# Largest value over the partitions by TensorE and VectorE in place of GpSimd's collective, in a chain of attention, Fourier transforms and two FFNs

## The chip, the cores and the metric

One core of one Trainium2 chip. The time is device microseconds (us) of one execution of the program; three runs of the kernel before gave 1623.56, 1623.72 and 1625.95, so 1623.72 is the median that everything is compared with. PE is TensorE, DVE VectorE, ACT ScalarE, POOL GpSimd, SP SyncE.

## The reference

```python
def _attn_ref(q, k, v):                       # 8 batches, 8 heads, 576 tokens, d = 64
    q_s = np.exp(q - np.max(q, axis=-1, keepdims=True))
    q_s = q_s / (np.sum(q_s, axis=-1, keepdims=True) + 1e-09)
    k_s = np.exp(k - np.max(k, axis=2, keepdims=True))
    k_s = k_s / (np.sum(k_s, axis=2, keepdims=True) + 1e-09)
    kv = np.einsum('bhsd,bhse->bhde', k_s, v)
    return np.einsum('bhsd,bhde->bhse', q_s, kv)

def _moe_ref(x, w_ch1, w_ch2):                # x: [8, 576, 512]
    u = x + np.real(np.fft.fft(np.fft.fft(x, axis=1), axis=2))
    mu = np.mean(u, axis=-1, keepdims=True)
    var = np.mean((u - mu) ** 2, axis=-1, keepdims=True)
    un = (u - mu) / np.sqrt(var + 1e-06)
    return u + np.maximum(un @ w_ch1, 0.0) @ w_ch2          # 512 to 2048 to 512

def _moe2_ref(x, mu_k, mu_r, w_k, w_v, w_r):
    x_prev = np.concatenate([np.zeros((B, 1, D)), x[:, :-1, :]], axis=1)
    xk = mu_k * x + (1.0 - mu_k) * x_prev
    xr = mu_r * x + (1.0 - mu_r) * x_prev
    k = np.maximum(xk @ w_k, 0.0)
    return 1.0 / (1.0 + np.exp(-(xr @ w_r))) * (k * k @ w_v)
```

The weights of the first FFN come as float64. The two maxima that matter here are the one of k over the sequence (`axis=2`), and one that the reference doesn't have: the largest weight of W1 and of W2, by which the kernel chooses a power of two to scale the weights with.

## The kernel before, in words

**Attention** goes by batch b and half hf (four heads each), sixteen halves, in `attention(b)`. In `kt` (k) the 128 partitions are rows of the sequence, so the largest k of a column is a maximum along the free dimension (`tensor_reduce` L313, and two small ones L316 for the last 64 rows) and then one over the partitions (L317, a collective of GpSimd, in place in `m`, all partitions get the result). Beside it q's softmax runs over d, in the free dimension: L321 maximum, L323 subtraction, L324 exponential, L333 to L337 the division by the sum. k less its maximum is L327 and L330, its exponential L331; L342 and L343 make k'v on TensorE in a PSUM bank, L345 to L353 divide it (`kvbd`), L376 transposes q, L395 multiplies q with `kvbd`, L396 writes the result to `U[b]`. Which halves use GpSimd for a subtraction is written in the tables POOL_Q (q less its largest) and POOL_K (k less its largest).

**Transform** (`transform(b)`): even and odd parts (L429 to L445), a product over the features (L474) and one over the sequence (L494 to L498, "stage 2"), whose results are added to `u` in L507 to L517. L517 is the last instruction of a batch's transform.

**Norm** (`norm(i)`): layer norm by blocks of 512 tokens, nine blocks; block 1 needs the transforms of batches 0 and 1. Block 0 goes in two parts of 256 tokens. For block 1 GpSimd adds (L571, L573, L589, L590) and multiplies with the reciprocal deviation (L623); L637 makes the low half of the f16 pair (`unh`, `unl`) that the products read.

**Weights**: `largest` finds the maximum of the absolute value of a piece along the free dimension (L193); `scales(w)` takes the maximum over the pieces (L202), the one over the partitions (L203, the collective again), and makes powers of two (L204 to L209). `split(w, c)` decodes a piece of float64 to float32 on VectorE and GpSimd (L229, L230, GpSimd's L232, L234) and writes two f16 parts (ACT's L243, L246 and L247; L244 on VectorE or L248 on GpSimd).

**FFN**: for each block 16 times `mm1` (L825, three f16 products) and `mm2` (L845), L830 and L831 between them, and L863 adds the result to `u`. In block 0 the products wait for the pieces of weights as they come.

**Order.** Three strands (attention; transform and norm; weights) are written as generators, of which `side()` takes a piece after every few products. The order on each engine comes from a scheduler with a timeline of its own, so the rows of an engine are not in the order of the code; each engine executes its rows in order. Marks (BEHIND_X, BEHIND_Z, BEHIND_S) hold pieces back behind a point of the first batch. Beside the products the strands have two PSUM banks (`side`); the first batch, before the products, also uses one of `acc0` to `acc3`. After the ninth block comes the last part (L887 to L913), which is products throughout.

Of the kernel before, what the change touches and what calls it, by code (L numbers as in the profile page):

```python
# [8 lines left out]
F32 = mybir.dt.float32  # L9
# [5 lines left out]
ALU = mybir.AluOpType  # L15
AX = mybir.AxisListType

S = 576          # tokens of a batch
DM = 512         # model width
HALF = 288       # S / 2  # L20
NK = 258         # cosine columns: k = 256, 0..255 and one of zeros
NS = 290         # s' = 0..288 and one of zeros
RAW = 3          # chunks of the last part's weights that are under way
# Halves (batch, half) of the attention whose steps GpSimd takes: q less its largest, q times its
# reciprocal sum, k less its largest; and halves and weights that come after a mark of the first batch.
POOL_Q = ((0, 0), (1, 0), (2, 0))
POOL_M = ((2, 0),)
POOL_K = ((0, 1), (1, 0))
# [3 lines left out]
# Blocks whose norm GpSimd multiplies, and blocks that are waited for least: their sums on TensorE and in float32.  # L32
# [3 lines left out]
# Rows j of the folded sequence, by tile, of the even and the odd part. The last tile of the even part  # L36
# starts with rows that the tile before has too, where its tables are zero.
JT = (((0, 128), (128, 128), (225, 64)), ((0, 128), (128, 128), (256, 32)))
# 2^-100, the high word of its float64 read as float32
# [4 lines left out]
def net(ctx, tc, q, k, v, w1, w2, mu_k, mu_r, w_k, w_v, w_r, ce_d, se_d, cs_d, ss_d, alt_d, id_d, out):  # L44
# [19 lines left out]
    def aside(first):  # L64
        """A bank beside the products; before those begin, one of theirs too."""
        if not first:
            return bank("side", 2)
        turn_of[0] += 1
        x = turn_of[0] % 6
        return bank("side", 2) if x in (0, 3) else bank(f"acc{(1, 2, 4, 5).index(x)}", 1)  # L70
# [3 lines left out]
    def segments(i):  # L74
        """The batches that a block of tokens covers: batch, first row, rows, place in the block."""
# [9 lines left out]
    # ------------------------------------------------------------------ pools of the first part  # L85
# [20 lines left out]
    ident = fc.tile([128, 128], F32, name="ident")  # L106
    ceh = fc.tile([128, 2, NK], F32R, name="ceh")
# [11 lines left out]
    def load_constants():  # L119
        # They pass where W1 will lie.  # L120
# [8 lines left out]
    def first_constants():  # L129
        st = fw.tile([128, NS], F32, tag="pc", name="st")[:, 0:128]  # L130
        nc.vector.memset(st, 1.0 / DM)
        nc.gpsimd.memset(wsc[:, 7:8], 1e-6)
# [9 lines left out]
    # ------------------------------------------------------------------ weights of the FFN  # L142
    def load_weight(pool, src, t, c, bufs):
        """256 columns of 128 rows of a float64 weight, as its words."""
# [903 lines left out]
```

## Time and profile before

| what | number |
|---|---|
| median of 3 runs | 1623.72 us |
| span of the profiled execution (first to last instruction) | 1622.4 us |
| own time of the profiled execution | not given; the median is 1.3 us above the span |
| PE busy | 1485.2 us (92%) |
| DVE busy | 885.7 us (55%) |
| ACT busy | 576.7 us (36%) |
| POOL busy | 181.8 us (11%) in 188 instructions |
| mean granted TensorE clock | 0.958 |

Busy shares are means over stages that differ: PE is at 26% to 60% of the slices in the first eighth of the span, then at 90% or more to the end. What a change in the first eighth is worth has to be read there, engine by engine, in order of time. One thing isn't counted as busy on POOL: before a collective and again before the next ordinary instruction the engine stands still (idle "<-issue", or put down to an instruction long done). In the program's order these places have an `ISA` row without operands.

### The profile page before, as it was taken

To read this page: it belongs to the slowest core of one execution; us is meant where nothing else is said; L and a number is where in the kernel's file an instruction comes from. 1 tells how busy PE (TensorE), PEld (TensorE's weight loads), DVE (VectorE), ACT (ScalarE), POOL (GpSimd) and SP (SyncE) were. 2 spreads that over 40 slices of the span, in tenths; PEclk is the share of its full clock that TensorE was granted. 3 is DMA by queue.
4 is the path that set the end of the run, shared out by engine and by line. 5 is a ranking of instruction groups with operands and counts; after the bars stand their busy time and mean duration, and the time that the engine had idled before them with its cause. 6 is when DMAs were issued, how large, how long until landed. Compare 5 with 4: busy or idle time off the path is not lost.

```text
span 1622.4 us, 17906 instructions
## 1 busy us (share of the span) xinstructions
PE 1485.2 (92%) x7044; PEld 944.9 (58%) x7044; DVE 885.7 (55%) x1473; ACT 576.7 (36%) x1010; POOL 181.8 (11%) x188
## 2 busy tenths in 40 slices
PE   2644667999999999999999989999999999999999
PEld 2533444454555555555555434446888888888887
DVE  3685879945647547546553896513334443434432
ACT  2563545423323323233232342313334333433421
POOL 1102535302010020020010210000000000000000
PEclk7766889999999999999999999999999999999999
DMA  8363333201201102102010232101001101100000
GB/s 351 130 227 122 133 109 135 87 1 46 72 1 58 61 1 72 46 6 84 30 52 1 97 109 80 52 1 52 26 27 52 48 5 52 53 26 26 27 26 26
DMA packets 41408, 105.99 MB, mean 65 GB/s; under 512 B 5323, under 2 KB 11628, under 8 KB 40300
## 3 DMA queue, kind: packets, MB, share of 16 engines
q1 hardware_dynamic: 41324, 104.85, 18.1%
q8 instruction: 55, 0.90, 0.2%
q14 instruction: 29, 0.24, 0.0%
HBM read 85.96 MB, written 18.87 MB: 65 GB/s over the span
## 4 chain that ended last, share of the span: by engine, by line
PE 76%; DVE 7%; issue 1%; POOL 1%; ACT 1%; DMA 1%; SPq 0%; DVEq 0%; ACTq 0%
PE h L825 19%; PE acc L845 18%; PE acc L913 12%; PE h L898 12%; PE h L887 6%; PE side L474 2%; PE side L494 2%; PE side L342 1%; PE side L395 1%; DVE eo L429 1%; DVE hl L831 1%; PE side L498 0%; PE side L376 0%; DVE words L230 0%; DVE u L863 0%
## 5 line engine op out<-in xcount | busy, mean ns | idle before, releaser
L825 PE MATMUL h<-unh,w1h 128*128 128x512 f16 (+1 forms) x608 | 226.9, 373 | 23.6 <-ACT w1h L247 20.3
L825 PE MATMUL h<-unh,w1l 128*128 128x512 f16 (+1 forms) x608 | 225.5, 373 | 24.0 <-POOL w1l L248 23.7
L825 PE MATMUL h<-unl,w1h 128*128 128x512 f16 (+1 forms) x608 | 226.8, 373 | 0.0
L845 PE MATMUL acc<-hl,w2h 128*128 128x512 f16 x576 | 220.3, 383 | 0.5 <-DVE hl L831 0.5
L845 PE MATMUL acc<-hh,w2l 128*128 128x512 f16 x576 | 219.9, 382 | 0.0
L845 PE MATMUL acc<-hh,w2h 128*128 128x512 f16 x576 | 212.8, 382 | 5.1 <-ACT hh L830 5.0
L825 PEld LDWEIGHTS <-w1h 128*128 128x128 f16 x1216 | 120.0, 99 | 154.6 <-ACT w1h L247 21.6
L845 PEld LDWEIGHTS <-w2h 128*128 128x128 f16 x1152 | 112.1, 99 | 137.9 <-issue 9.5
L913 PE MATMUL acc<-wvh,kk 128*128 128x512 f32 x576 | 190.6, 395 | 0.0
L831 DVE SCALAR_TENSOR_TENSOR hl<-h,hh 128x512 f16<-128x512 f32 x144 | 98.7, 686 | 166.7 <-ACT hh L830 166.1
L898 PE MATMUL h<-x,wkh 128*128 128x512 f32 x576 | 180.8, 395 | 0.0
L830 ACT ACTIVATE hh<-h 128x512 f16<-128x512 f32 x144 | 85.1, 592 | 227.9 <-PE h L825 227.6
L903 DVE SCALAR_TENSOR_TENSOR ke<-h,ke 128x512 f32<-128x512 f32 x72 | 49.7, 690 | 177.8 <-ACT ke L902 177.7
L913 PEld LDWEIGHTS acc<-wvh,kk 128*128 128x128 f32 x576 | 108.1, 188 | 26.3
L898 PEld LDWEIGHTS h<-x,wkh 128*128 128x128 f32 x576 | 108.1, 188 | 26.2
L913 PE MATMUL acc<-wvl,kk 128*128 128x512 f32 x288 | 113.7, 395 | 0.0
L898 PE MATMUL h<-x,wkl 128*128 128x512 f32 x288 | 113.7, 395 | 0.0
L825 PEld LDWEIGHTS <-w1l 128*128 128x128 f16 x608 | 60.1, 99 | 88.5 <-POOL w1l L248 25.6
L902 ACT ACTIVATE ke<-h 128x512 f32<-128x512 f32 x72 | 42.9, 596 | 175.8 <-PE h L898 175.8
L845 PEld LDWEIGHTS <-w2l 128*128 128x128 f16 x576 | 56.8, 99 | 66.2 <-issue 3.3
L887 PE MATMUL h<-wrh,x 128*128 128x512 f32 x288 | 92.1, 396 | 0.0
L699 DVE TENSOR_TENSOR x<-aa,x 128x512 fp32r<-128x512 f32 x72 | 47.8, 687 | 72.0 <-PE h L887 62.4
(290 smaller groups left out, 2251.9 us busy)
## 6 DMA issues: line engine op xcount, KB each, us to landing
raw<-in_w_dram SPq DMA_DIRECT2D x22, 512.0 KB, 3.4
vt<-in_v_dram SPq DMA_DIRECT2D x16, 650.0 KB, 5.8
kt<-in_k_dram SPq DMA_DIRECT2D x16, 576.0 KB, 4.0
qt<-in_q_dram SPq DMA_DIRECT2D x16, 576.0 KB, 3.7
out_dram<-oo SPq DMA_DIRECT2D x36, 256.0 KB, 2.2
y<-yT SPq DMA_DIRECT2D x8, 1026.0 KB, 5.0
w2h<-in_w_dram SPq DMA_DIRECT2D x8, 1024.0 KB, 7.4
w2l<-in_w_dram SPq DMA_DIRECT2D x8, 1024.0 KB, 8.3
```

Source lines behind the costliest of these rows:

```text
L474: mm(out=pt, lhsT=a[:, e, g, js], rhs=c[:, g, :], start=first, stop=(e == 1 and g == 1 and a is el))
L494: mm(out=pt, lhsT=a[:, i, cols], rhs=c[:, i, :], start=(i == 0 and c is ch and a is yh), stop=False)
L699: nc.vector.tensor_tensor(out=l[:, t, 0:n], in0=a, in1=h[:, t, 0:n].bitcast(F32), op=ALU.subtract)
L825: mm(out=pt[:, o:o + m], lhsT=a[:, t, fs], rhs=c[:, t, o:o + m], start=(t == 0 and a is w1h and c is xh), stop=(t == 3 and a is w1l))
L830: nc.scalar.activation(out=hh[:, 0:n], in_=pt[:, 0:n], func=AF.Relu)
L831: nc.vector.scalar_tensor_tensor(out=hl[:, 0:n], in0=pt[:, 0:n], scalar=0.0, in1=hh[:, 0:n], op0=ALU.max, op1=ALU.subtract)
L845: mm(out=acc[x][:, 0:n], lhsT=a[:, f, xs], rhs=c[:, 0:n], start=(f == 0 and a is w2h and c is hh), stop=(f == NF - 1 and a is w2l))
L887: mm(out=pt[0:m, :], lhsT=a[:, t, o:o + m], rhs=c[:, t, :], start=(t == 0 and a is rh and c is wrh), stop=(t == 3 and a is rl))
L898: mm(out=pt[:, 0:n], lhsT=a[:, t, fs], rhs=c[:, t, 0:n], start=(t == 0 and a is wkh and c is kh), stop=(t == 3 and a is wkl))
L902: nc.scalar.activation(out=kr[:, 0:n], in_=pt[:, 0:n], func=AF.Relu)
L903: nc.vector.scalar_tensor_tensor(out=kr[:, 0:n], in0=pt[:, 0:n], scalar=0.0, in1=kr[:, 0:n], op0=ALU.max, op1=ALU.mult)
L913: mm(out=acc[x][0:m, :], lhsT=a[:, o:o + m], rhs=c[:, f, :], start=(f == 0 and a is h2 and c is wvh), stop=(f == NFK - 1 and a is l2))
```

## The change

For batches 0, 1 and 2 (`MAX_PE`) the maximum of k over the partitions is no longer a collective. Two TensorE transposes bring `m` (128 x 256) into a PSUM bank with the columns on the partitions; VectorE takes the maximum along the free dimension (128 x 2); VectorE multiplies an identity matrix with these (128 x 256, two diagonal matrices); a product with a matrix of ones gives every partition all 256 maxima, in the other half of the same PSUM bank, where the subtraction reads them. GpSimd can't do that subtraction here, so POOL_K is empty: the k subtractions of halves (0, 1) and (1, 0) move from GpSimd to VectorE. `scales` does the same in three steps: a diagonal matrix from the 128 maxima, the product with ones, and a maximum along the free dimension. Batches 3 to 7 keep the collective. A new 128 x 128 tile `one` and its memset are added; comments are dropped.

```diff
-POOL_K = ((0, 1), (1, 0))
+POOL_K = ()
...
+MAX_PE = (0, 1, 2)
...
     ident = fc.tile([128, 128], F32, name="ident")
+    one = fc.tile([128, 128], F32, name="one")
...
         nc.vector.memset(st, 1.0 / DM)
+        nc.vector.memset(one, 1.0)
...
         nc.vector.tensor_reduce(out=m, in_=amax[:, w, :], axis=AX.X, op=ALU.max)
-        nc.gpsimd.partition_all_reduce(out_ap=inv, in_ap=m, channels=128, reduce_op=bass_isa.ReduceOp.max)
+        dg = fw.tile([128, NS], F32, tag="pc", name="dg")[:, 0:128]
+        ts(out=dg, in0=ident, scalar1=m, scalar2=None, op0=ALU.mult)
+        pt = aside(False)[:, 0:128]
+        mm(out=pt, lhsT=one, rhs=dg, start=True, stop=True)
+        nc.vector.tensor_reduce(out=inv, in_=pt, axis=AX.X, op=ALU.max)
...
-            nc.gpsimd.partition_all_reduce(out_ap=m, in_ap=m, channels=128, reduce_op=bass_isa.ReduceOp.max)
+            if b in MAX_PE:
+                pt = aside(b == 0)
+                for x in range(2):
+                    nc.tensor.transpose(out=pt[:, 128 * x:128 * x + 128], in_=m[:, 2 * x:2 * x + 2, :], identity=ident)
+                mx = wsc[:, 2:6:3, None]
+                nc.vector.tensor_reduce(out=mx[:, :, 0], in_=pt[:, 0:256].rearrange("p (x c) -> p x c", x=2), axis=AX.X, op=ALU.max)
+                dg = m.rearrange("p h d -> p (h d)").rearrange("p (x c) -> p x c", x=2)
+                tt(out=dg, in0=ident[:, None, :].to_broadcast([128, 2, 128]), in1=mx.to_broadcast([128, 2, 128]), op=ALU.mult)
+                mm(out=pt[:, 256:512], lhsT=one, rhs=dg.rearrange("p x c -> p (x c)"), start=True, stop=True)
+                m = pt[:, 256:512].rearrange("p (h d) -> p h d", h=4)
+            else:
+                nc.gpsimd.partition_all_reduce(out_ap=m, in_ap=m, channels=128, reduce_op=bass_isa.ReduceOp.max)
```

The scheduler orders the engines anew. Three places follow; the changed kernel's lines are 21 further down in the attention (L327 there is L348, L345 is L366), 9 in `split` (L232 is L241, L248 is L257) and 21 after that.

On GpSimd, from the first collective of the first batch to the weights. Before, the first three halves:

```order
L317 ISA
L317 ISA m<-m 128x256
L323 ISA
L323 TENSOR_TENSOR qt<-qt,st 128x1152
L317 ISA
L317 ISA m<-m 128x256
L327 ISA
L327 TENSOR_TENSOR kt<-kt,m 128x1024
L330 TENSOR_TENSOR kt<-kt,m 64x128 x2
```

In the change, from its first such row to the fourth of the weights:

```order
L344 ISA
L344 TENSOR_TENSOR qt<-qt,st 128x1152 x2
L592 TENSOR_TENSOR sq<-u 128x2x64
L241 TENSOR_TENSOR dec<-dec,raw 128x512
L241 TENSOR_TENSOR words<-words,raw 128x512
L241 TENSOR_TENSOR words<-words 128x512
L257 TENSOR_TENSOR w1l<-dec,w1h 128x512
```

One ISA row is left ahead of the weights; the next ones stand at the first collective of batch 3.

On VectorE, the second half of the first batch, in the change (L332 and L334 are the new maximum and the new diagonal matrices, L366 the first step of the division of k'v, L345 before):

```order
L354 TENSOR_REDUCE st<-qt 128x18
L355 TENSOR_SCALAR st<-st 128x18
L356 RECIPROCAL st<-st 128x18
L358 TENSOR_TENSOR qt<-qt,st 128x1152
L332 TENSOR_REDUCE wsc<-acc_199 128x2
L334 TENSOR_TENSOR m<-ident,wsc 128x256
L348 TENSOR_TENSOR kt<-kt,acc_199 128x1024
L351 TENSOR_TENSOR kt<-kt,acc_199 64x128 x2
L366 TENSOR_SCALAR rk<-acc_217 128x2
```

Before, L337 (now L358) was followed by L345 at once: the k subtraction was GpSimd's. Now it stands behind q's division.

On VectorE, the end of the second batch's transform. Before, it lies among the pieces of weights (L244, L229, L230) and block 0's products (L831):

```order
L244 SCALAR_TENSOR_TENSOR w1l<-words,wsc,w1h 128x512
L229 TENSOR_SCALAR dec<-raw 128x512
L507 TENSOR_TENSOR sd<-pc,side 128x290
L508 TENSOR_TENSOR sd<-pc,side 128x290
L229 TENSOR_SCALAR words<-raw 128x512
L230 SCALAR_TENSOR_TENSOR dec<-raw,dec 128x512
L510 TENSOR_TENSOR u<-u,sd 128x2x289
L511 TENSOR_TENSOR u<-u,sd 128x2x287
```

In the change it comes after the last L831 of block 0 (L852 there) and the first two L863 (L884):

```order
L852 SCALAR_TENSOR_TENSOR hl<-h,hh 128x512
L884 SCALAR_TENSOR_TENSOR u<-acc_694,wsc,u 128x512
L884 SCALAR_TENSOR_TENSOR u<-acc_695,wsc,u 128x512
L528 TENSOR_TENSOR sd<-pc,side 128x290
L529 TENSOR_TENSOR sd<-pc,side 128x290
L332 TENSOR_REDUCE wsc<-side 128x2
L884 SCALAR_TENSOR_TENSOR u<-acc_696,wsc,u 128x512
L334 TENSOR_TENSOR m<-ident,wsc 128x256
```

All pieces of weights stand ahead of it. On TensorE stage 2 of the second batch (L494, now L515) likewise comes behind all of block 0's products, among half of which it stood before.

## Rows read from the trace of the kernel before

**Rows 1.** Busy time in stretches: engines, PE clock, DMA share, GB/s
```profile
121.00:152.00 31.00, 7.13 (x39) 5.95 (x40) 14.92 (x34) 7.11 (x10) 9.25 (x9) 0.61 0.17 55
152.00:268.00 116.00, 87.32 (x494) 56.36 (x493) 96.25 (x140) 60.52 (x106) 52.89 (x35) 0.87 0.43 154
...
960.00:1622.00 662.00, 658.64 (x2878) 475.43 (x2877) 273.06 (x453) 224.58 (x380) 6.35 (x64) 1.00 0.11 38
```

**Rows 2.** PE's timeline: first products of block 0 and block 1
```profile
133.34 0.39 PE L825 MATMUL h<-unh,w1h 128*128 128x256 f16 x1 [20.07 <-ACT w1h L247]
...
311.45 0.38 PE L825 MATMUL h<-unh,w1h 128*128 128x512 f16 x1
```

**Rows 3.** PE's waits, 100 to 320 us: total, times, longest
```profile
PE h L825 <- POOL w1l L248: 23.7, 2, 12.2
PE h L825 <- ACT w1h L247: 20.3, 2, 20.1
```

**Rows 4.** GpSimd's timeline, the first batch
```profile
11.25 1.08 POOL L317 PARTITION_ALL_REDUCE m<-m  x1 [9.92 <-issue]
23.18 2.11 POOL L323 TENSOR_TENSOR qt<-qt,st 128x1152 f32<-128x1152 f32 x1 [10.85 <-issue]
35.35 1.08 POOL L317 PARTITION_ALL_REDUCE m<-m  x1 [10.07 <-issue]
43.51 2.33 POOL L327 TENSOR_TENSOR kt<-kt,m 128x1024 f32<-128x1024 f32 x1 [7.07 <-issue]
```

**Rows 5.** DVE's timeline: q's sum (0,0), k'v (0,1), last of block 0, last of transform 1
```profile
26.52 1.35 DVE L333 TENSOR_REDUCE st<-qt 128x18 f32<-128x1152 f32 x1 [9.86 <-ACT qt L324]
...
52.77 0.16 DVE L345 TENSOR_SCALAR rk<-side 128x2 f32<-128x2 f32 x1 [0.45 <-PE side L343]
...
119.96 0.67 DVE L637 TENSOR_TENSOR unl<-d,unh 128x512 f16<-128x512 f32 x1
...
266.48 1.71 DVE L517 TENSOR_TENSOR u<-u,sd 128x574 f32<-128x574 f32 x1
```

**Rows 6.** DVE's waits, 0 to 320 us: total, times, longest
```profile
DVE wsc L204 <- POOL wsc L203: 11.3, 2, 5.9
DVE words L229 <- POOL w1l L248: 10.8, 2, 5.5
DVE kt L327 <- POOL m L317: 9.3, 3, 4.9
DVE w1l L244 <- ACT w1h L243: 5.3, 2, 4.8
DVE dec L229 <- POOL w2l L248: 4.6, 1, 4.6
```

**Rows 7.** GpSimd's timeline, around the collectives of batches 1 and 3
```profile
122.28 1.53 POOL L317 PARTITION_ALL_REDUCE m<-m  x1 [11.51 <-DVE m L316]
130.60 1.26 POOL L232 TENSOR_TENSOR dec<-dec,raw 128x512 uint32<-128x512 uint32 x1 [6.79 <-DVE qt L323]
...
280.56 1.53 POOL L317 PARTITION_ALL_REDUCE m<-m  x1 [7.01 <-DVE m L316]
```

**Rows 8.** Prices: DVE's groups by form, 100 to 320 us (busy, mean ns)
```profile
L831 DVE SCALAR_TENSOR_TENSOR hl<-h,hh 128x512 f16<-128x512 f32 x17 | 11.4, 678 | 1.1 <-ACT hh L830 0.9
...
L313 DVE TENSOR_REDUCE m<-kt 128x256 f32<-128x1024 f32 x5 | 9.6, 1918 | 0.0
...
L327 DVE TENSOR_TENSOR kt<-kt,m 128x1024 f32<-128x1024 f32 x4 | 4.9, 1218 | 5.4 <-POOL m L317 5.4
...
L440 DVE TENSOR_TENSOR eo<-eo 128x289 f32<-128x289 f32 x8 | 3.3, 432 | 0.0
```

**Rows 9.** GpSimd's and DVE's timelines at 174 us, side by side
```profile
174.17 2.11 POOL L323 TENSOR_TENSOR qt<-qt,st 128x1152 f32<-128x1152 f32 x1
174.23 2.33 DVE L229 TENSOR_SCALAR dec<-raw 128x512 uint32<-128x512 uint32 x1 [4.59 <-POOL w2l L248]
...
120.56 0.41 DVE L229 TENSOR_SCALAR dec<-raw 128x512 uint32<-128x512 uint32 x1
```

## The prediction

> **What bounds the kernel now.** I read the busy time in stretches first, then the waits of the engines in the stretches that aren't full. From 960 us on TensorE is busy 658.6 of 662 us [rows 1], and it stays at about 99% from some 315 us: nothing that this change touches lies there, so those 1311 us can only be moved, not shortened. The gain or loss must arise before block 1's first product, at 311.45, which waited for nothing [rows 2]. Between 121 and 152 us TensorE is busy 7.1 of 31 us, at a clock of 0.61; between 152 and 268 it is busy 87 of 116 us while VectorE is busy 96, the fullest engine [rows 1]. The reader is to see a chain of VectorE up to 268 us, with TensorE waiting beside it.
>
> TensorE's own waits say for what: block 0's first product came at 133.34 after 20.1 us on the high half of W1, and 23.7 us went on the low halves that GpSimd writes [rows 2, 3]. GpSimd's timeline says why: every change between the collective and ordinary instructions leaves it standing, some 10 us in the first 36 us (9.92, 10.85, 10.07) and about 7 later (7.07, 6.79, 7.01) [rows 4, 7], while the collective itself takes 1.08 to 1.53 us. I call these gaps loads: in the program's order an ISA row stands at each. VectorE's waits name the same source: 11.3 us for the scales' collective, 10.8 and 4.6 for buffers that GpSimd frees late, 9.3 for k's maximum and 5.3 for ScalarE's w1h [rows 6].
>
> **The change part by part.** I follow VectorE through four points: k'v of half (0, 1) (L345, at 52.77), the last L637 of block 0 (119.96, done at 120.6), the first product (133.34), and the last L517 of the second batch (266.48, done at 268.2) [rows 2, 5].
>
> *The head.* Before, two loads lay ahead of q's subtraction of (0, 0) at 23.18, and two more ahead of the k subtraction at 43.51 [rows 4]. Now one load is left, for the q subtraction itself: it starts where the collective did, 11.3, thus 11.9 earlier, and L333 with it, at 14.6 instead of 26.52 [rows 5]. Then VectorE works in order: 6.1 us of (0, 0) as before, some 4.6 for the maximum, subtraction and exponential of q of (0, 1) (three operations at the 1.35 of L333 or a little less), 3.6 for L333 to L337, which gives 28.9. The maximum and the k subtraction stand behind that. Nothing in the trace shows the new chain; its nearest rows are L440, 0.43 us for 128x289, for each of its two VectorE steps, and 0.39 us for a product of 256 columns [rows 2, 8]. With two TensorE steps that is 1.7 us without and up to 3 us with latencies; I take 2.3, and 1.8 for the subtraction (L327's 1.22 and two of L330): 33.0. What follows the k subtraction until L345 took 6 us before (52.77 less 43.51, less the 3.3 of the subtraction). So L345 comes at about **39.5**, 13 earlier. Bounds: all three loads gone from a pure chain and the rest 11.9 earlier would give 23.7; only one of them off the path, 42.7.
>
> *To the last L637 of block 0*: 67.9 us before. The scale's wait goes (5.4 of the 11.3 [rows 6]; 0.6 of new work comes), and about 4.5 us of the second batch move behind it (one L313 at 1.92 and six small ones at L440's 0.43 [rows 8]). 58.5 remain: T = **98** instead of 120.6.
>
> *To the first product*: 12.7 before, of which 6.79 were the load ahead of L232 [rows 7]. What is left is decode, scaling and rounding, 5 us: **103** instead of 133.3.
>
> *To the end of the transform.* Before, 147.6 us (120.6 to 268.2). VectorE's waits in it that come from loads: 5.9 for the second scale, 10.8 and 4.6 for late buffers, 4.8 of the 5.3 on w1h, 4.9 of the 9.3 on k's maximum [rows 6]: 31 go. Added to VectorE: 4 halves at 0.85 (two steps at 0.43), 0.6 for the scale, 1.8 for half (1, 0)'s k subtraction: 5.7. The 4.5 moved behind come back. And in the new order stage 2 stands behind all pieces of weights and block 0's products: some 15 instructions of 128x512 at 0.68 [rows 8] pass ahead of it, 10 us. That makes 147.6 - 31 + 5.7 + 4.5 + 11 = 138, so the last L517 ends at **236 to 240** instead of 268.2. The pieces go faster for GpSimd too; VectorE stays the fullest engine (96 of 116 us), so I count no more than its own waits.
>
> *Block 1.* Before, its norm took 43.3 us from L517 to the first product, wholly beside block 0's products [rows 2, 5]. Now these are done before, and TensorE stands in the meantime. The chain keeps two loads: the collective of batch 3 stands in it with 7 us on either side [rows 7], since that batch isn't in MAX_PE. I get 41 us (36 if the loads fall beside other steps, 45 if GpSimd's adds queue behind them), and 2 us for products at a lower clock after the gap, as at 0.61 in the stretch before the first product [rows 1]. Block 1 begins at 238 + 41 = 279; its first product then counts as if at about 279.5 against 311.45. That is 32 us.
>
> *The other edits.* TensorE does 20 more small products (about 8 us at most) before 315 us, where it idles; the memset of `one` and the wider use of a bank fall in waits of 10 us at the head. VectorE's extra work, some 10 us in all, is in the sums above. SP's queue gets and loses nothing; loads of q, k and v leave when their buffers come free, which is earlier. The cover for the TensorE work is GpSimd's loads: where they go, it is VectorE's work that covers it.
>
> The sum: the span of 1622.4 less 32 is 1590.4; the median lies 1.3 above the span, so **1591 us** is the time (1591.7 from the sum, rounded down).
>
> The collective's own time is 1.08 to 1.53 us, the new chain's 1.7 to 3: by instruction times alone the change would lose. The Trainium skill says as much: "GPSIMD Engine Reference", section 4.1 "Engine selection", names GpSimd for a reduction along the partition dimension and not VectorE. By that rule the eight replaced collectives would cost about 1.2 us more each. This trace disagrees as far as it goes: 7 to 10 us stand beside each collective here, which the rule doesn't count.
>
> **The rivals.**
> - *More gain.* VectorE's simple operations took 0.41 us alone and 2.33 beside GpSimd [rows 9]; the means of the weights' stage lie between. If, with fewer waits, fewer of them meet, up to 18 us come off the 138: 1573.
> - *Less gain.* The head is set by VectorE and by the arrival of q, k and v rather than by loads: T near 110, or the two `side` banks, of which the maxima of batches 1 and 2 now hold one from the transposes to the subtraction, make products of the transform wait. 12 to 24 of the 32 us go: 1603 to 1615.
> - *The loads were hidden.* If the waits pass on to others (DMA, ScalarE's exponentials), nothing but the order changes: 1620 to 1627. Against it: the load of 6.79 ends at the very instruction whose result TensorE waits for [rows 3, 7].
> - *Only the instructions count.* Six halves and two scales at 1.2 us more each (the chain's middle of 2.4 less the collective's 1.2), on VectorE's path: 9.6 more, 1633.
> - *Slower by a lock.* A VectorE operation that meets a GpSimd instruction with two inputs waits for its end (0.41 against 2.33 [rows 9]). GpSimd has about 64 us of such instructions between T and the last L517; they spread now over a shorter time in which VectorE has no idle places. Some 18 us of it are in today's durations, so at most 46 come on top: L517 at 284, block 1 at 325, time 1637. It decides from 33 of the 46 on; below that the change still wins. The Trainium skill has such a rule: "SBUF — State Buffer", section "Who interferes with whom", has VectorE and GpSimd share a port pair that one instruction holds exclusively. The row at 174.23 agrees; how often they meet isn't shown.
>
> **How the numbers follow.** The forecast (1580 to 1602) gets 0.52, more gain 0.15, less gain 0.22, loads hidden 0.04, instructions only 0.02, the lock 0.05. Faster is the first three, 0.89; same 0.04; slower 0.07 (about 0.2%, 3.2 us, is what a measurement of this kernel can tell from no change). The range from 1568 to 1612 takes in the first two, with their bounds, and most of the third; about 0.18 is left out.
>
> **What would show it.** In the profile of the changed kernel: GpSimd's first ordinary instruction at 11 to 13 us and no gap of 7 us until batch 3's collective; L345's successor of (0, 1) near 39; last low half of block 0 near 98; first product near 103, and no wait of 12 us for low halves; last transform instruction of batch 1 near 238; a wait of 30 us or more on TensorE between block 0's and block 1's products; block 1 at 276 to 284; from there the same 1311 us. A first product before 95 or after 115, a block 1 after 300, or a later part that isn't 1311 us would each prove a step wrong.

## The result, and the profile after

The changed kernel takes 1606.43 us (median of 4 runs, 1604.72 to 1608.45) against 1624.84 of the kernel before in the same runs: a ratio of 0.9882, 95% interval 0.9865 to 0.9898. That is faster by 18 us, clear of the scatter, where 32 were forecast; the time lies inside the range of 1568 to 1612, but above the 1580 to 1602 of the forecast itself, where the rival "less gain" (1603 to 1615) was put. The profiled execution has a span of 1602.9 us and took 1604.7; the span before was 1622.4, so 19.5 us went. TensorE is busy 1489.3 us (1485.2 before), which leaves 113.6 us in which it isn't, against 137.2.

First the busy time in the stretches of [rows 1] (engines PE, PEld, DVE, ACT, POOL, then clock, DMA share, GB/s):

```profile
121.00:152.00 31.00, 21.30 (x118) 14.25 (x115) 29.93 (x47) 15.70 (x25) 13.61 (x10) 0.83 0.41 133
152.00:268.00 116.00, 94.62 (x488) 54.62 (x486) 90.57 (x139) 54.64 (x97) 36.32 (x26) 0.94 0.35 121
268.00:315.00 47.00, 33.84 (x158) 20.35 (x159) 32.39 (x51) 16.84 (x30) 11.76 (x6) 0.79 0.12 40
...
960.00:1602.00 642.00, 639.15 (x2788) 466.61 (x2786) 248.90 (x392) 214.57 (x358) 6.11 (x62) 1.00 0.10 33
```

The hole of 121 to 152 us, with 7.1 us of TensorE, is closed (21.3). A new one stands further on. Here the same view in the stretches that matter now:

```profile
190.00:220.00 30.00, 27.88 (x141) 15.93 (x141) 22.75 (x38) 18.27 (x33) 13.97 (x11) 0.96 0.54 182
220.00:241.00 21.00, 21.00 (x103) 10.99 (x102) 7.62 (x12) 5.73 (x11) 0.07 (x1) 1.00 0.00 1
241.00:253.00 12.00, 10.57 (x67) 8.27 (x65) 9.72 (x19) 3.61 (x5) 0.13 (x1) 1.00 0.24 90
253.00:290.00 37.00, 14.85 (x50) 7.86 (x51) 30.38 (x46) 16.16 (x28) 15.35 (x8) 0.65 0.29 99
```

Up to 220 us every piece of the weights is done (GpSimd's last low half ends at 220.1); from there to 241 TensorE alone is full, at its upper clock, while VectorE is busy 7.6 of 21 us. Then, from 253 to 290, TensorE is busy 14.9 of 37 us and its mean granted clock is 0.65: block 1's norm runs with nothing beside it. TensorE's timeline, with block 0's first product, the start of the second batch's stage 2, the wait in block 1's norm, and block 1's first products (before: [rows 2]):

```profile
100.17 0.40 PE L846 MATMUL h<-unh,w1h 128*128 128x256 f16 x1
...
235.44 0.49 PE L515 MATMUL side<-csh,yh 128*128 128x290 f32 x1
...
274.62 2.08 PE L575 MATMUL side<-sq,onesr 128*128 128x512 f32 x2 [10.44 <-POOL sq L611]
...
287.27 1.01 PE L846 MATMUL h<-unh,w1h 128*128 128x512 f16 x2 [1.27 <-ACT unh L657]
289.47 0.59 PE L846 MATMUL h<-unl,w1h 128*128 128x512 f16 x1 [1.19 <-DVE unl L658]
```

VectorE's timeline, at the points that the prediction follows (before: [rows 5]; L354 was L333, L366 was L345, L658 was L637, L538 was L517; L332, L334 and L348 are the new chain and the k subtraction behind it):

```profile
9.10 2.11 DVE L334 TENSOR_TENSOR m<-ident,wsc 128x256 f32<-128x256 f32 x1
12.53 1.22 DVE L348 TENSOR_TENSOR kt<-kt,acc 128x1024 f32<-128x1024 f32 x1 [1.31 <-PE acc L335]
...
16.13 1.35 DVE L354 TENSOR_REDUCE st<-qt 128x18 f32<-128x1152 f32 x1
...
27.60 0.42 DVE L332 TENSOR_REDUCE wsc<-acc 128x2 f32<-128x256 f32 x1
28.05 0.43 DVE L334 TENSOR_TENSOR m<-ident,wsc 128x256 f32<-128x256 f32 x1
30.36 1.22 DVE L348 TENSOR_TENSOR kt<-kt,acc 128x1024 f32<-128x1024 f32 x1 [1.88 <-PE acc L335]
...
35.87 0.16 DVE L366 TENSOR_SCALAR rk<-acc 128x2 f32<-128x2 f32 x1 [3.79 <-PE acc L364]
...
93.87 0.68 DVE L658 TENSOR_TENSOR unl<-d,unh 128x512 f16<-128x512 f32 x1
...
241.01 1.41 DVE L884 SCALAR_TENSOR_TENSOR u<-acc,wsc,u 128x512 f32<-128x512 f32 x2 [6.39 <-PE acc L866]
...
252.04 0.75 DVE L538 TENSOR_TENSOR u<-u,sd 128x574 f32<-128x574 f32 x1
```

And GpSimd's timeline (before: [rows 4, 7]). The first row waited for VectorE and not for itself; the next gaps at a collective, of 6 and 7 us, stand around batch 3's collective, in the middle of block 1's norm (L594 and L610 are its sums, L573 and L589 before):

```profile
8.82 2.12 POOL L344 TENSOR_TENSOR qt<-qt,st 128x1152 f32<-128x1152 f32 x1 [7.49 <-DVE st L342]
...
255.31 1.36 POOL L594 TENSOR_TENSOR sq<-sq 128x512 f32<-128x512 f32 x1
262.69 1.08 POOL L338 PARTITION_ALL_REDUCE m<-m  x1 [6.02 <-issue]
270.90 2.33 POOL L610 TENSOR_TENSOR sq<-sq 128x1024 f32<-128x1024 f32 x1 [7.13 <-ACT qt L345]
```

So the head and the weights gained what was forecast or more: block 0's first product came 33 us earlier. But block 1 began only 22 to 24 us earlier, as the second batch's transform ended at 252.8 (15 us earlier than before, where 30 were forecast).

### The profile page after: what moved, and what is told of

Read it like the earlier page. It is cut to its first block, busy times and chain, and to the rows that moved or that the text cites. A ratio compares the mean times of both kernels' runs of the same rounds, so it can differ in the third digit from the quotient of the medians.

```text
span 1602.9 us, 17944 instructions
## 1 busy us (share of the span) xinstructions
PE 1489.3 (93%) x7072; PEld 945.5 (59%) x7072; DVE 893.8 (56%) x1496; ACT 579.1 (36%) x1010; POOL 164.8 (10%) x174
## 4 chain that ended last, share of the span: by engine, by line
PE 78%; DVE 14%; DMA 3%; issue 2%; ACT 2%; POOL 1%; SPq 0%; DVEq 0%; POOLq 0%; ACTq 0%
PE acc L866 18%; PE h L846 18%; PE acc L934 13%; PE h L919 13%; PE h L908 6%; PE side L495 2%; PE side L515 2%; DMA raw<-in_w_k_dram 1%; PE side L416 1%; PE side L363 1%; DMA raw<-in_w_dram 1%; DVE words L239 1%; DVE m L322 1%; DVE top L197 1%; DVE eo L450 1%
## 5 line engine op out<-in xcount | busy, mean ns | idle before, releaser
L852 DVE SCALAR_TENSOR_TENSOR hl<-h,hh 128x512 f16<-128x512 f32 x144 | 98.9, 688 | 179.5 <-ACT hh L851 178.6
L924 DVE SCALAR_TENSOR_TENSOR ke<-h,ke 128x512 f32<-128x512 f32 x72 | 49.7, 690 | 177.5 <-ACT ke L923 177.4
```

Of the source, the lines that this page charges most:

```text
L852: nc.vector.scalar_tensor_tensor(out=hl[:, 0:n], in0=pt[:, 0:n], scalar=0.0, in1=hh[:, 0:n], op0=ALU.max, op1=ALU.subtract)
L924: nc.vector.scalar_tensor_tensor(out=kr[:, 0:n], in0=pt[:, 0:n], scalar=0.0, in1=kr[:, 0:n], op0=ALU.max, op1=ALU.mult)
```

## The experiments

Three theories were set against each other. **A**: what the change removes is GpSimd standing still at each switch between collective and ordinary work, and what is missing against the forecast is an order in which the second batch's transform, and with it block 1's norm, come too late. **B**: the collective's own time is all there was, and the new order brings the gain. **C**: VectorE bounds that stage anyway, and another order only moves work. All runs in one table; "not busy" is the span less TensorE's busy time, "transform" is the end of the second batch's transform, "block 1" the first product of block 1.

| kernel | us (median) | ratio to before, 95% | span | not busy | transform | block 1 |
|---|---|---|---|---|---|---|
| before | 1624 to 1626 | 1 | 1622.4 | 137.2 | 268.2 | 311.5 |
| the change | 1606.4 | 0.9882 (0.9865 to 0.9898) | 1602.9 | 113.6 | 252.8 | 287.3 |
| e1 scales only | 1625.6 | 1.001 (1.000 to 1.002) | 1624.0 | 132.7 | 267.4 | 315.3 |
| e2 maxima only | 1598.9 | 0.9843 (0.9829 to 0.9858) | 1596.6 | 103.0 | 248.8 | 282.9 |
| e3 weights held | 1617.7 | 0.9955 (0.9939 to 0.997) | 1615.1 | 119.5 | 228.8 | 307.2 |
| e4 before, no switch in the head | 1618.9 | 0.9968 (0.9958 to 0.9977) | 1617.9 | 127.2 | 266.9 | 308.9 |
| e5 change, third batch held | 1599.6 | 0.9845 (0.9831 to 0.986) | 1594.9 | 106.5 | 220.2 | 250.5 |
| e6 maxima only, third batch held | 1595.9 | 0.9826 (0.981 to 0.9841) | 1594.7 | 102.5 | 217.1 | 248.2 |
| e7 four batches | 1598.2 | 0.9837 (0.982 to 0.9854) | 1598.4 | 105.9 | 254.8 | 284.6 |
| e8 eight batches | 1633.2 | 1.0055 (1.004 to 1.007) | 1631.2 | 125.2 | 255.5 | 285.3 |
| e9 before, third batch held | 1637.7 | 1.0076 (1.0062 to 1.0089) | 1637.7 | 145.3 | 226.7 | 306.2 |
| e10 maxima only, milder hold | 1592.9 | 0.98 (0.9787 to 0.9814) | 1590.4 | 102.1 | 226.6 | 262.0 |
| e11 as e10, four batches | 1601.8 | 0.9853 (0.9839 to 0.9866) | 1600.9 | 103.5 | 224.5 | 262.5 |
| e12 change, milder hold | 1600.0 | 0.9848 (0.9833 to 0.9864) | 1596.6 | 104.4 | 228.6 | 261.9 |

### e4: the kernel before, without a switch in the head

```diff
-POOL_Q = ((0, 0), (1, 0), (2, 0))
-POOL_K = ((0, 1), (1, 0))
+POOL_Q = ((1, 0), (2, 0))
+POOL_K = ((1, 0),)
```

> The kernel before, all collectives kept; only the subtraction of q's maximum of half (0,0) and of k's maximum of half (0,1) move from GpSimd to VectorE, so that GpSimd's first three instructions after the memsets are collectives with no ordinary work between. Theory A: no switch is left between them, so the second collective runs at once when its data is there (about 20 us instead of 35), k'v of half (0,1) is divided near 38 to 42 us instead of 52.8, and block 0's last low half comes near 108 instead of 120; time 1608 to 1616. Theory B (the time beside a collective is its own, whatever stands around it): second collective still some 10 us after the first's end or more, head within 3 us of before, time 1621 to 1627.

Measured: 1618.9. This is the direct test of what a collective costs, and GpSimd's timeline of this kernel answers it (in brackets how long the engine stood, and for what; "issue" is nothing that the profile shows):

```profile
13.20 1.08 POOL L317 PARTITION_ALL_REDUCE m<-m  x1 [11.88 <-issue]
20.10 1.06 POOL L317 PARTITION_ALL_REDUCE m<-m  x1 [5.81 <-DVE m L316]
51.59 1.06 POOL L317 PARTITION_ALL_REDUCE m<-m  x1 [30.43 <-DVE m L316]
59.68 2.38 POOL L327 TENSOR_TENSOR kt<-kt,m 128x1024 f32<-128x1024 f32 x1 [7.03 <-issue]
```

Two collectives without ordinary work between them need no pause: the second starts when VectorE's m is there, at 20.1 instead of 35.4 [rows 4]. The 7.03 us come back where an ordinary instruction follows the third. In the head this kernel is even ahead of the change (k'v of half (0,1) divided at 34.2 us against 35.9, and 52.8 before [rows 5]), by moving two subtractions and no collective. So A holds for the head and B falls, though the time is 3 us above what A expected (1608 to 1616). The second reading is as important: block 0's last low half is ready 20 us earlier than before (100.4 against 120.6), and 5 us of that are left in the time, because the end of the second batch's transform hardly moved (266.9). What the head gains isn't worth its length.

### e1 and e2: the change in two halves

e1 is the kernel before with the new `scales` alone, e2 the change with the old `scales`:

```diff
-MAX_PE = (0, 1, 2)
-POOL_K = ()
+MAX_PE = ()
+POOL_K = ((0, 1), (1, 0))
```

```diff
-        dg = fw.tile([128, NS], F32, tag="pc", name="dg")[:, 0:128]
-        ts(out=dg, in0=ident, scalar1=m, scalar2=None, op0=ALU.mult)
-        pt = aside(False)[:, 0:128]
-        mm(out=pt, lhsT=one, rhs=dg, start=True, stop=True)
-        nc.vector.tensor_reduce(out=inv, in_=pt, axis=AX.X, op=ALU.max)
+        nc.gpsimd.partition_all_reduce(out_ap=inv, in_ap=m, channels=128, reduce_op=bass_isa.ReduceOp.max)
```

> Only the two scales go over TensorE and VectorE; all maxima of k stay collectives, and the two k subtractions are back on GpSimd. Theory A (what the change removes is GpSimd standing still at each switch between collective and ordinary work): the two scale collectives take four switches with them, so VectorE loses its 11.3 us of waiting on the scales and some of the 15 us on buffers that GpSimd frees late; the head stays as before (last step of k'v of half (0,1) near 52.8 us). Some 8 to 12 us less, 1612 to 1617. Theory B (the collective's own time is all there was, the gain of the change comes from the new order): within 3 us of 1624.

> Only the maxima of k of batches 0 to 2 go over TensorE and VectorE; the two scales stay collectives. Theory A: the head is as in the change (k'v of half (0,1) divided near 36 us, against 52.8 before), and the scales' two collectives cost their switches of 7 us again, about 90 to 110 us, where the first weights wait for GpSimd: first product 7 to 14 us later than the change's 100, time 1608 to 1615. Theory B: as the change, 1606, within 3 us.

Measured: 1625.6 and 1598.9; A missed on both, in opposite directions (1625.6 is the number of B, 1598.9 is neither's). The scales alone bring nothing, and the maxima alone bring 7.6 us more than the whole change (1606.4). In e1 block 0's first product comes 18 us earlier than before, but the k subtraction of the second batch's second half, which was at 125.0 before, waits for a collective that now stands behind the first weights (at 141.4 us, 122.3 before [rows 7]), and the transform ends where it did. TensorE's timeline of e1, and VectorE's:

```profile
115.01 0.39 PE L846 MATMUL h<-unh,w1h 128*128 128x256 f16 x1 [18.66 <-ACT w1h L256]
```

```profile
142.52 1.23 DVE L348 TENSOR_TENSOR kt<-kt,m 128x1024 f32<-128x1024 f32 x1 [4.68 <-POOL m L338]
...
266.64 0.75 DVE L538 TENSOR_TENSOR u<-u,sd 128x574 f32<-128x574 f32 x1
```

In e2 it is the other way: block 0's first product comes 8 us later than in the change, the second batch's k'v 12 us earlier (97.8 against 109.9), and the transform ends 4 us earlier (248.8); block 1 begins 4.4 us earlier, a good half of the 7.6. TensorE and VectorE in e2:

```profile
108.53 0.39 PE L842 MATMUL h<-unh,w1h 128*128 128x256 f16 x1 [6.44 <-ACT w1h L252]
...
282.89 0.74 PE L842 MATMUL h<-unh,w1h 128*128 128x512 f16 x2 [1.34 <-ACT unh L653]
```

```profile
97.77 0.15 DVE L362 TENSOR_SCALAR rk<-side 128x2 f32<-128x2 f32 x1
...
248.04 0.75 DVE L534 TENSOR_TENSOR u<-u,sd 128x574 f32<-128x574 f32 x1
```

What gets early with new scales are the weights, and here they aren't what block 1 waits for: the second batch is.

### e3: hold the weights

In the change, the pieces of the last third of the weights are held behind the last instruction of the second batch's transform:

```diff
-        if b == 0:
-            mark(4, mv, ma)
+        if b < 2:
+            mark((4, 7)[b], mv, ma)
...
-                split(1, 4 * g - 2 + z)
+                with behind(7 if g == 3 else None):
+                    split(1, 4 * g - 2 + z)
...
-                split(0, 4 * g + z)
+                with behind(7 if g == 3 else None):
+                    split(0, 4 * g + z)
```

(and in block 0 the strands advance twice as fast, so that the mark is there when the pieces come; e3 is two edits at once).

> The change with another order: the last third of the weights' pieces is held behind the end of the second batch's transform on VectorE and ScalarE, so that its second stage and block 1's norm no longer come behind all of block 0's products. Theory A (the part of the gain that is missing against the prediction, 12 us, is TensorE standing between 248 and 288 us while block 1's norm runs): the transform ends near 215 instead of 252.8, the norm runs beside the last 55 us of block 0's products, block 1 begins at 255 to 270 instead of 289, time 1572 to 1590. Rival C (VectorE is the bound of that stage anyway, shared with GpSimd, and the held pieces only come later): 1600 to 1610.

Measured: 1617.7, slower than the change by 11 and outside both expectations. The transform ends 24 us earlier (228.8), and block 1 begins 20 us later (307.2). VectorE had nothing else to do while it waited for the transform's pieces, and the weights were missing after. Busy time from 190 to 228 us, and TensorE's timeline:

```profile
190.00:228.00 38.00, 31.67 (x150) 21.01 (x151) 18.30 (x30) 12.82 (x23) 0.00 (x0) 0.87 0.14 49
```

```profile
262.27 0.61 PE L848 MATMUL h<-unh,w1h 128*128 128x512 f16 x1 [7.27 <-ACT w1h L252]
...
305.02 0.39 PE L868 MATMUL acc<-hh,w2l 128*128 128x512 f16 x1 [3.20 <-POOL w2l L257]
```

Both views are of e3. VectorE is busy 18.3 of these 38 us, and GpSimd not at all. An early transform isn't enough: the weights have to fill the places that it leaves.

### e5, e6 and e9: hold the third batch

VectorE works almost without a pause from 95 to 190 us in the change (busy 87.3 of the 92 us from 98 on), and the third batch's first half stands in that time ahead of the second batch's transform. Here the weights stay, and the third batch's attention waits for the end of that transform (marked as in e3):

```diff
-BEHIND_X = {(1, 0): 4, (1, 1): 4}
+BEHIND_X = {(1, 0): 4, (1, 1): 4, (2, 0): 7, (2, 1): 7}
...
+            while b == 2 and done_dft[0] < 1:
+                yield -1
             nxt = after(b, hf)
```

e5 is the change with this, e6 is e2 with this, e9 is the kernel before with this.

> The change, with the attention of the third batch held behind the last instruction of the second batch's transform (the weights are not held). Theory A' (VectorE works without a pause from 95 to 217 us in the change, and the third batch's first half stands in that time ahead of the second batch's transform, for which block 1 waits; the order, not a lack of engine time, leaves TensorE standing from 248 to 288): the transform ends at 220 to 235 instead of 252.8, block 1's norm runs beside block 0's last products, without a collective in it, block 1 begins at 258 to 275 instead of 289, time 1576 to 1594. Rival C (what is held comes back: the third batch is then late for block 2 and TensorE stands there instead): block 1 early as said, but TensorE short of work after 300 us and the time 1600 to 1610.

> The kernel with the maxima alone (scales as collectives, 1598.9) and the same hold of the third batch. Theory A': the scales on TensorE lost 7.5 us only by the order that they brought (weights ahead of the second batch's attention); with the third batch held that matters less, so this comes within 5 us of the run with the whole change and the hold, at 1576 to 1596. Rival D (the scales' steps on TensorE and VectorE cost by themselves): this is 7 us or more faster than that run, as without the hold.

> The kernel before, all collectives kept, with the hold of the third batch's attention behind the second batch's transform that was put on the change before. Theory A' (block 1 waits for the second batch's transform; what stands ahead of it on an engine counts, in either kernel): the transform ends 10 to 20 us earlier than 268.2, but block 0's products, which wait for the weights, end near 311 as before and block 1 cannot begin before them: at most 5 us less, 1619 to 1625. If the order alone were worth what the maxima on TensorE brought, it would be at 1600 to 1612.

e5 measured 1599.6: block 1 began 37 us earlier than in the change (250.5), beyond what was expected, and 7 us of that reached the end, 5.6 us above the expected range. The first half of theory A is shown, and so is the loss that rival C named: most of what was won came back as a longer rest. From block 1's first product to the end of the span the change took 1315.6 us, e5 1344.4. Busy time in e5 after block 1 began:

```profile
315.00:400.00 85.00, 79.92 (x401) 43.35 (x399) 48.20 (x73) 28.32 (x50) 14.41 (x9) 1.00 0.11 35
400.00:600.00 200.00, 194.97 (x998) 106.64 (x997) 115.13 (x182) 63.35 (x109) 21.43 (x15) 0.99 0.14 48
600.00:800.00 200.00, 195.85 (x1005) 107.44 (x1004) 110.81 (x166) 64.34 (x115) 19.02 (x14) 1.00 0.10 34
```

The change has 199.8 or more of 200 us in the last two of these stretches. TensorE's waits from 315 us to the end name the norms' f16 halves (3.8 us of them at 369 and 373 us, at the start of block 2, which needs the third batch) and q of the last three batches (588 to 812 us); they add up to 24 us, against 11 in the change. So 13 of the 29 us are new waits. Another 13 are TensorE's busy time, which from block 1 on is longer (1312.4 against 1299.7 us): 11.1 us of attention's products stood in the hole of 253 to 290 in the change, and such products now stand in time that is full. TensorE's waits in e5, 315 us to the end (total, times, longest):

```profile
PE h L848 <- ACT unh L659: 6.3, 3, 3.1
PE side L399 <- DVE qTl L394: 5.6, 3, 1.9
PE h L848 <- DVE unl L660: 4.5, 4, 2.5
```

e6 measured 1595.9, 3.7 us from e5 and within the 5 of the expectation; with the hold, the scales cost less, and as the runs of the two overlap (1594.6 to 1598.2 against 1596.7 to 1600.4), this rest is hardly clear of the scatter. e9 measured 1637.7, 12 us slower than before, where 5 less were the most that was thought of. Its transform ended at 226.7, 41 us earlier, by order alone. But block 1 began at 306.2, behind block 0's products, which wait for GpSimd as long as before: 26.5 us on its low halves, [rows 3] have 23.7. TensorE's waits in e9, 95 to 320 us:

```profile
PE h L827 <- POOL w1l L248: 26.5, 4, 11.7
PE h L827 <- ACT w1h L247: 23.9, 3, 21.3
```

From there to the end it took 20 us more than before (1331.5 against 1310.9), 12 us of it in TensorE's waits (21 us after 315 us, 8 before). So an early transform by order alone isn't the gain. It takes both: without the switches the weights come early enough for an early transform to be worth something.

### e7 and e8: four batches, eight batches

```diff
-MAX_PE = (0, 1, 2)
+MAX_PE = (0, 1, 2, 3)
```

and (0, 1, 2, 3, 4, 5, 6, 7).

> The change with batch 3's maxima on TensorE and VectorE too, so that no collective stands between GpSimd's additions of block 1's norm. Theory A: the additions of the squares begin when ScalarE's squares are there, near 265 instead of 270.9 us, block 1 begins 5 to 7 us earlier, time 1598 to 1602. Rival (VectorE's new work of 2 us for each half falls into the same chain): within 2 us of 1606.

> The change with all eight batches' maxima on TensorE and VectorE. Batches 4 to 7 lie where TensorE is 99% busy, so their products and transposes (three for each half, about 0.9 us of TensorE) come straight on top: 8 halves, 7 us more than the run with four batches, 1604 to 1610. If a collective's switches cost there too: the same as with four batches or less, 1595 to 1602.

e7 measured 1598.2, 8 us less than the change, at the lower end of the expected range. GpSimd's timeline has no switch in block 1's norm any more:

```profile
257.27 1.36 POOL L594 TENSOR_TENSOR sq<-sq 128x512 f32<-128x512 f32 x1
266.93 2.76 POOL L610 TENSOR_TENSOR sq<-sq 128x1024 f32<-128x1024 f32 x1 [8.29 <-ACT sq L607]
```

The squares are added as soon as ScalarE has them. In the change they were there at 264.9, and the sum began 6.0 us later, at 270.90. ScalarE's timeline of the change:

```profile
263.86 1.04 ACT L607 ACTIVATE sq<-d 128x1024 f32<-128x1024 f32 x1
```

From the transform's end to that sum it is 12.1 us in e7, where the change took 18.1 (270.90 less 252.8). But the transform ended 2 us later, and block 1 began only 2.7 us earlier (284.6 against 287.3; 5 to 7 were expected): where the rest of the 8 us lies isn't shown. e8 is the other end: 1633.2, 35 us more than e7 and slower than the kernel before. 7 were expected. TensorE is busy 13.5 us longer than in e7 (1506.0 against 1492.5) and not busy 19.3 us longer (its waits after 315 us are 26 us in all, against 6 in e7). TensorE's waits in e8, 315 us to the end: total, times, longest:

```profile
PE h L846 <- DVE unl L658: 5.8, 3, 3.7
PE side L581 <- ACT hl L579: 5.0, 2, 4.4
PE side L335 <- DVE m L334: 4.7, 2, 3.0
...
PE h L846 <- ACT unh L657: 4.2, 3, 2.7
```

4.7 us are waits of the chain itself, for the diagonal matrices; most (15.0) are the norms' parts. The chain's work on TensorE was sized well enough (8.8 us for the 8 halves), what it does to the full stage around it wasn't; which of the two (VectorE's work, or the `side` bank that a half keeps) makes the norms late was not told apart.

### e10, e11 and e12: a hold between

The mark stands behind the last step of the first product stage of the second batch's transform, not behind its end; e10 is on e2, e11 adds the fourth batch, e12 is on the whole change.

```diff
-        if b == 0:
-            mark(3, mv, ma)
+        if b < 2:
+            mark((3, 7)[b], mv, ma)
...
-BEHIND_X = {(1, 0): 4, (1, 1): 4}
+BEHIND_X = {(1, 0): 4, (1, 1): 4, (2, 0): 7, (2, 1): 7}
...
+            while b == 2 and done_att[0] == 1 and 7 not in marks:
+                yield -1
             nxt = after(b, hf)
```

> The kernel with the maxima alone, the third batch's attention held behind the first product stage of the second batch's transform only, a milder hold than behind its end (there block 1 began at 250 us instead of 285, and 28 of those 35 us were lost again behind, as TensorE waited for the norms and the third batch between 315 and 800 us). Theory E (block 1's early start and the third batch's lateness pay for each other; a hold between loses less): block 1 at 252 to 265, waits of TensorE after 315 us 5 to 10 us less, time 1586 to 1594. Otherwise within 3 us of 1596 and 1599, the full hold and none.

> As the run before, with batch 3's maxima on TensorE and VectorE too. With the third batch held, batch 3's collective no longer stands in block 1's norm, so the 8 us that four batches brought in the change are not there again: within 4 us of the run before. A gain of 6 us or more would say that the switch costs wherever it stands.

> The whole change, scales on TensorE and VectorE too, with the milder hold of the third batch, which gave 1592.9 with the scales as collectives. If the scales' part loses only by the order that it brings (weights ahead of the second batch's attention, whose first k'v is divided at 110 us instead of 98), the hold does not mend that: second batch's transform 3 to 10 us later than 226.6, time 1594 to 1600, as without the hold (7.5 us apart) and with the full hold (3.7). If the difference was chance in the order: within 2 us of 1592.9.

e10 measured 1592.9, the fastest of all: 0.98 of the kernel before (0.9787 to 0.9814), 13.5 us less than the change. Block 1 begins at 262.0, and TensorE's waits after 315 us add up to 19 us, 5 less than in e5. Theory E holds by each of its numbers, if narrowly by the time: the full hold (e6) is only 3.0 us slower, though the runs of the two don't overlap. e11 measured 1601.8, 9 us slower than e10, which neither side had expected; block 1 begins at the same time (262.5), so the loss lies behind it. In the two profiles TensorE's waits after 315 us are nearly alike (21 and 19 us), but in e11 it is busy 9.1 us longer in all (1497.4 against 1488.3), in places at a lower granted clock (0.83 against 1.00 from 580 to 600 us); what caused this stays open. The 8 us of e7, too, belong to its place, or to the new order that came with the edit; the runs don't part the two. e12 measured 1600.0, 7 us slower than e10, as the first case said, but not by its mechanism: the transform is 2 us later, not 3 to 10, and block 1 begins as early (261.9). The scales' part costs 7.6, 3.7 and 7.1 us in the three pairs that differ in nothing else; where those 7 us lie with the milder hold stays open. Every edit makes the scheduler order the engines anew, and in e11 one that was expected to be worth nothing went with 9 us: differences of that size between two kernels are shown here as times, and as causes only where a row shows the wait.

## Why the prediction was right, and where it was wrong

Right were the sign, the range, and the mechanism up to block 0's first product; the way from there to block 1 was not. That the time lies in the range is in part luck: it lies where "less gain" was put, whose mechanism didn't come about, and block 0's last low half, 3.4 us earlier than forecast, and a norm 4.8 us shorter made up for a part of the way to the transform's end, which took 20 us more (158.2 against 138). By its own points:

| point | before | forecast | measured |
|---|---|---|---|
| k'v of half (0, 1) | 52.8 | 39.5 | 35.9 |
| last L637 of block 0, done | 120.6 | 98 | 94.6 |
| block 0's first product | 133.3 | 103 | 100.2 |
| last L517 of the second batch, done | 268.2 | 236 to 240 | 252.8 |
| block 1, after the transform (steady products) | 43.3 | 41.5 | 36.7 |
| from there to the end of the span | 1310.9 | 1311 | 1313.4 |

**The head** went better than forecast by 3.6 us. The step "one load is left, for the q subtraction itself: it starts where the collective did, 11.3" was wrong: it started at 8.82, when VectorE's maximum was there. The price of the chain was right in size: from the first new VectorE step to the k subtraction 2.76 us in half (0, 1) against 2.3 taken (bounds 1.7 to 3), and 3.88 in half (0, 0), where L334 took 2.11 beside GpSimd's subtraction.

**VectorE's waits on loads** went as listed: of the 41 us in [rows 6] 2.5 are left after (1.1 us and 0.4 on w1l, and 1.0 on batch 3's maximum, which is still a collective). The new chain's own waits, 3.2 us at L348 for the product with ones and 0.8 at L212, took a part of their place; others came that the sum didn't have, and the next step failed by them.

**The step that failed** is "147.6 - 31 + 5.7 + 4.5 + 11 = 138", the way to the last L517, which took 158.2 us: longer than before, and not 10 us shorter. It was costed on VectorE alone, as "VectorE stays the fullest engine". Busy time over that way, before and after (VectorE is the third engine):

```profile
120.60:268.20 147.60, 94.65 (x532) 62.39 (x533) 111.78 (x175) 67.83 (x117) 62.15 (x43) 0.81 0.38 133
94.60:252.80 158.20, 129.71 (x710) 80.93 (x710) 130.59 (x207) 78.35 (x133) 59.62 (x42) 0.92 0.41 138
```

VectorE's work was sized well: 18.8 us more, where 5.7 + 4.5 + 11 were taken. What failed is the "- 31". Those waits went, but for some 2 us, and others took their place, and VectorE still idles 27.6 us (35.8 before): 6.4 us for TensorE at L884, 6.0 for ScalarE's half of block 0's results at L852, 4.8 for loads of the weights, 2.8 for ScalarE at L505. The order had stage 2 behind nearly all of block 0's products (the last of them ran at 243.7), and I priced that by the 15 VectorE instructions that pass ahead of it. TensorE had to do those products: from 220 to 241 us it is full, and VectorE waits. So stage 2 began at 235.44, only 1.5 us earlier than before, whatever had come earlier ahead of it. TensorE's timeline of the kernel before:

```profile
236.90 0.48 PE L494 MATMUL side<-csh,yh 128*128 128x290 f32 x1
```

The 15 us that the transform did gain lie behind that: 17 us from stage 2 to its end, 31 before, when it stood among the weights' pieces. That the prediction's own figure wasn't out of reach is shown by e5: with the third batch held, stage 2 began at 204.1 and the transform ended at 220. It is order and not lack of engine time; and e4 shows that the head and the weights can come 20 us earlier and the transform hardly move (266.9 against 268.2).

**The norm** came out 4.8 us shorter (36.7 against 41.5, inside its bounds of 36 to 45), and its collective between gaps of 6 and 7 us was where it was said to be; e7 puts 6 us of it on the switches. The "hole" in which TensorE stands was in the forecast, and at the right length, but 15 us later. The three differences, 14.8 - 4.8 + 2.4, are the 12.5 us between the forecast span (1590.4) and the measured one (1602.9), but for rounding. Three slips in the sums are small: 33.0 and 6 make 39.0 and not 39.5, the passes are 10 us in the text and 11 in the sum, and of the 2 us for a lower clock only 0.5 came into the 279.5.

Of the rivals, "less gain" had the number, not the mechanism: the head was not late, T was early, and in the whole span TensorE waited only once, 0.6 us, for a k subtraction (L351) that kept a `side` bank. **Loads hidden** and **instructions only** are out by the time and by e4. **The lock**: the row of L334 at 9.10, which took 2.11 us (0.43 at 28.05) and ends just after GpSimd's subtraction, shows it once more, and the section "Who interferes with whom" of the Trainium skill's "SBUF — State Buffer" agrees with it. But it didn't grow: the 64 instructions of L229 and L230 take 49.7 us after and 48.9 before. The rival wasn't put to its full test, as the stretch in which the two engines could meet got longer (158.2 us) and not shorter. The other rule cited, GpSimd for a reduction over partitions ("GPSIMD Engine Reference", section 4.1 "Engine selection", of the Trainium skill), holds here under a condition that the runs show: with no ordinary work between collectives GpSimd is as quick (e4's head, 34.2 us against 35.9), and with all eight batches taken off it the kernel is slower than before (e8), by more than the chain's own instructions.

What was not weighed at all is that a part which is faster by itself (the scales) can lose by what it moves forward. The sum counted the 11.3 us of waiting for the scales as gain; e1 and e2 put that part at 1.5 us lost, hardly clear of the scatter, and 7.6 us lost.

## What to carry to other kernels

Before adding up waits that go, follow the one chain on which the next full stage starts (here attention, transform and norm of the second batch) and cost each of its steps on every engine whose queue it stands in, TensorE too. What a faster part sends forward may stand ahead of that chain in an engine's order, so measure the parts of a change one by one: here one half alone was 7.6 us better than the whole, and a hold of the third batch brought 6 more. A custom operation that makes GpSimd stand at each switch is cheap among its like; count the switches, not the operations.

## What the runs showed of the hardware that was not expected

- GpSimd's first ordinary instruction didn't stand for anything but its data (8.82 us, 7.49 of waiting for VectorE), while the first collective started at 11.25 and, in e4, at 13.20. Of the first two collectives in a row the second waited only for its data (5.81 us for VectorE's m).
- A longer chain on a full TensorE costs more than its own instructions: in e8 the chain's products and transposes came to 9.8 us after 315 us (18 records of products, 6.1 us, and 18 of transposes, 3.7 us; e7 has 1.0 us there), and the time rose by 35 against e7.
- In the hole of 253 to 290 us, where TensorE was busy 14.9 of 37 us, its granted clock was 0.65 on average, a mix of its two levels (1.2 and 2.4 GHz), and block 1's product at 289.47 took 0.59 us, against 0.38 for such a one in [rows 2]. The forecast had 2 us for this; the stretch after the first product is 2.4 us longer than before.
